# A retention layer and a gated FFN on one core: chunk 4's first and chunk 5's second pair of batches as row tiles, and a new order from chunk 3's end

## The chip, the cores and the metric

The kernel runs on one core of one Trainium2 chip. The metric is the device time of one execution in microseconds (us); the time of a kernel is the median of several runs. Beside the runs there is one profiled execution with a trace of every instruction.

Engines are named as the profile names them: PE is TensorE (matrix products), PEld its loading of the stationary operand, DVE is VectorE, ACT is ScalarE, POOL is GpSimd, SP is SyncE. SP and POOL also issue the transfers.

## The reference

Two stages follow each other. The first is a linear recurrence over 768 positions, for 4 batches and 8 heads of width 64, each head with its own decay:

```
for t in range(S):
    state = gamma * state + k[:, :, t] (outer) v[:, :, t]
    y[:, :, t] = scale * q[:, :, t] @ state
```

The second takes the 3072 rows of 512 values and computes `rms-norm(x) * rms_g`, then `silu(xn @ w_gate) * (xn @ w_val) @ w_out` with an inner width of 1536. Inputs and output are float32; the kernel multiplies in bfloat16.

## The kernel before

The 768 positions are cut into 6 chunks of 128. A chunk c with its 4 batches b is one group of 512 rows: the recurrence is done chunk by chunk, and the FFN of a chunk follows while the recurrence of the next runs in between.

The order of the work is written out by hand. `ORDER` is one long text of words, and the loop at the end calls one small function for each word, in that order; each engine then carries out its own instructions in the order in which they were recorded. A word is a name, then numbers, then `@` with an engine (D, A, P, S for DVE, ACT, POOL, SP) or `/` with the PSUM banks that its products are written to, one digit for each bank. PSUM has eight banks, 0 to 7. A product into a bank waits until the last reader of what stood in that bank is done.

The words that matter here, with c and b as first numbers:

- `Lq`, `Lk`, `Lv` load q, k and v; `Cq` multiplies q by its decay and casts it, `V` does so for v; `tq`, `tk` are transposes on the way of a transfer, issued by SP, that give qT and kT. In chunks 0 and 1 `Tq`, `Tk` transpose on PE and `Eq`, `Ek` copy the result out.
- `A` (L393 to L402) makes the scores of one or two batches, 64 rows of the array high, two heads beside each other in two banks per batch; `M0`, `M1` mask them (L423). `mc` (L276) makes the mask of chunk 1, one half on POOL, one on DVE.
- `Y` (L429 to L443) makes the chunk's output in one bank: 8 products of the masked scores with v, then 4 products of qT with the state `st_b`, 128 rows high.
- `Z` (L405 to L416) makes only the products of qT with the state, for two batches at once, as 16 products 64 rows high that alternate between two banks. Each of the two banks then holds half of the heads of both batches. `Y` with a third number adds the products with v to them (L433). Before, only chunk 4's second pair is done this way.
- `S`, `R`, `N` are the rms norm: squares on ACT, the root on POOL, the scaling on DVE. For a batch that went through `Z`, S and N are two instructions each and R has one more (L452, L464, L476).
- `XE` transposes the normed rows into `xnT`, through SP in the later chunks.
- `K`, `U`, `B` bring the state up to date: products (L525), sum on DVE (L534), cast on POOL (L541).
- `g`, `v` are the FFN's two first products for one of the 12 column blocks (`g.c.n0.n1.b0.b1`, L549), `s` the Silu on ACT (L560), `h` the product with it on DVE (L568, into `hT`).
- `d` is the last product (L575), `e` a part of it for the last batch (L597), `o` the copy out of PSUM (L140), `st` the store (L588).
- `D` (L514) scales k in the first two chunks; `wg`, `wv`, `wo` load the weights through POOL; `H` are products that only keep PE busy at the start.

Rings of buffers in SBUF (the `bufs` in the code) hold an instruction back where its buffer is still in use: 3 for the Silu's result, 4 for `xn`, 6 for `o_sb`.

Of the kernel before, what the change touches and what calls it, by code (L numbers as in the profile page):

```python
# [17 lines left out]
Lk.0.2@S H.4/4 yd causal Lv.0.2@S>causal yt rms.1@S ident Ck.0.2@A Lq.0.0@P H.8/1 Lq.0.1@P Lq.0.2@P Tk.0.2/7 H.3/5  # L18
Lk.0.0@P Tq.0.1/0 vd Tq.0.0/4 Ek.0.2@D Lk.0.1@P Tq.0.2/1 Lk.0.3@P G/7 V.0.2@D Eq.0.1@D Tk.0.0/0 Tk.0.1/6 Eq.0.2@D
Eq.0.0@D iota Lq.0.3@P A.0.2/31 Lv.0.1@P mk0 Lv.0.0@P Lv.0.3@P Ek.0.0@D mk1 GE@A wg.0.2 M1.0.2 wv.0.2 H.2/4 M0.0.2  # L20
Ek.0.1@A A.0.0/5270 D.0.2@P M1.0.1 Tk.0.3/6 Y.0.2/1 Tq.0.3/0 M0.0.1 H.2/4 tab Lk.1.1@P M1.0.0 M0.0.0 S.0.2 Ek.0.3@A
J.0.0/4 J.0.1/7 R.0.2 Y.0.1/2 Eq.0.3@A S.0.1 H.1/6 H.3/0 H.1/5 D.0.0@D Y.0.0/3 N.0.2 J.0.3/5 D.0.1@D wv.2.4 R.0.1
X.0.2/6 N.0.1 S.0.0 wg.2.4 A.0.3/41 R.0.0 X.0.1/0 XE.0.2@A wg.4.6 D.0.3@D M0.0.3 XE.0.1@A g.0.0.2.2.3/2 K.0.2.2/5
K.0.0.2/6 M1.0.3 U.0.2.2@A s.0.0.2.2.3 N.0.0 v.0.0.2.2.3/7 g.0.0.2.1.2/0 h.0.0.2.2.3 Y.0.3/5 Lq.1.0@P wv.4.6 X.0.0/3
U.0.0.2@A S.0.3 wg.6.9 Tk.1.1/4 v.0.0.2.1.2/2 XE.0.0@D s.0.0.2.1.2 h.0.0.2.1.2 g.0.0.2.0.1/6 R.0.3 wv.6.9 Ek.1.1@A
v.0.3.4.0.3/3 v.0.2.3.0.3/4 N.0.3 g.0.3.4.0.3/0 Lk.1.2@P s.0.0.2.0.1 X.0.3/6 v.0.0.2.0.1/5 XE.0.3@A Lk.1.0@P B.0.0
wg.9.12 s.0.3.4.0.3 Lq.1.1@P g.0.5.6.0.3/1 g.0.2.3.0.3/7 h.0.3.4.0.3 s.0.2.3.0.3 Lq.1.2@P h.0.2.3.0.3 g.0.4.5.0.3/0
# [5 lines left out]
g.0.9.10.0.4/4 s.0.9.10.0.4 B.0.2 g.0.10.11.0.4/2 s.0.10.11.0.4 Ek.1.0@D A.1.0/3710 M1.1.1 A.1.2/46 v.0.10.11.0.4/2
v.0.11.12.0.4/0 M0.1.2 M0.1.1 v.0.9.10.0.4/5 M0.1.0 Lv.2.0@S d.0.0.0.4/1 M1.1.0 M1.1.2 h.0.9.10.0.4 Y.1.1/3
d.0.3.0.4/6 Lk.2.3@P h.0.11.12.0.4 Y.1.0/4 S.1.1 Lk.1.3@P R.1.1 h.0.10.11.0.4 S.1.0 N.1.1 d.0.1.0.4/0 R.1.0
d.0.2.0.4/5 N.1.0 X.1.1/3 d.0.2.4.8 d.0.0.4.8 Lv.1.3@P d.0.3.4.8 X.1.0/7 d.0.3.8.12 XE.1.0@A Y.1.2/2 Tq.1.3/7
d.0.0.8.12 S.1.2 d.0.1.4.8 Lq.2.0@S XE.1.1@D o.0.0@A Eq.1.3@D o.0.3@A R.1.2 N.1.2 Tk.1.3/1 d.0.2.8.12 X.1.2/3 Ek.1.3@A
Lk.2.2@P D.1.3@D Lq.2.1@S A.1.3/17 XE.1.2@A M1.1.3 K.1.0/4 K.1.2.2/6 K.1.1/2 B.0.3 M0.1.3 Lq.2.2@S tk.2.2 Lk.2.0@P
g.1.0.1.0.3/3 v.1.2.3.0.3/7 U.1.1@D Y.1.3/1 s.1.0.1.0.3 g.1.1.2.0.3/3 S.1.3 Lk.2.1@P g.1.3.4.0.3/2 o.0.2@A R.1.3
U.1.2.2@D d.0.1.8.12 Cq.2.1@P s.1.3.4.0.3 U.1.0@D g.1.2.3.0.3/2 v.1.0.1.0.3/5 N.1.3 Lq.3.1@S s.1.1.2.0.3 X.1.3/3  # L40
h.1.0.1.0.3 tk.2.0 v.1.3.4.0.3/1 Lk.3.1@P tq.2.1 v.1.1.2.0.3/5 B.1.2 XE.1.3@D h.1.3.4.0.3 s.1.2.3.0.3 h.1.2.3.0.3
h.1.1.2.0.3 g.1.9.10.0.4/4 v.1.9.10.0.4/6 tk.2.3 v.1.0.4.3.4/7 g.1.8.9.0.4/2 Cq.2.0@P Lq.2.3@S o.0.1@D s.1.9.10.0.4
# [30 lines left out]
tk.5.2 Y.4.3.2 Y.4.2.2 S.4.1 h.3.7.8.0.4 v.3.11.12.0.4/7 U.4.0.2@D V.5.1@A tk.5.3 Lv.5.3@S d.3.0.0.10/3 S.4.2 XE.4.0@S
h.3.11.12.0.4 S.4.3 Cq.5.0@P d.3.0.10.12 tq.5.1 R.4.3 N.4.3 o.3.0@A tq.5.0 d.3.2.0.12/1 R.4.1 d.3.1.0.10/2 o.3.2@A
tk.5.1 R.4.2 B.4.0 N.4.1 XE.4.3@S N.4.2 XE.4.2@S V.5.0@D B.4.1 A.5.2/3514 d.3.1.10.12 d.3.3.0.12/6 XE.4.1@S M1.5.2
g.4.8.9.0.4/0 tk.5.0 B.4.3 M1.5.3 M0.5.2 v.4.8.9.0.4/4 o.3.3@D V.5.3@P s.4.8.9.0.4 B.4.2 Y.5.2/5 M0.5.3 o.3.1@A
# [560 lines left out]
```

## Time and profile before

| what | value |
|---|---|
| median of 3 runs | 232.57 us (232.56 to 232.95) |
| profiled execution | 231.72 us |
| its span (first to last instruction) | 230.0 us |
| PE busy | 224.5 us, 98% of the span |
| granted TensorE clock | 1.00 |
| DVE, POOL, ACT busy | 127.3, 105.4, 84.1 us |

In rows of the profile, "L549 PE MATMUL g_ps<-xnT,wg_b 128*128 128x512 x4" is line 549, engine, operation, what is written from what, the size of the stationary tile (rows * columns), the size of the moving operand and how many instructions the row holds. In a stretch in order of time the first two figures are the start and the length in us, and a bracket names the idle time ahead and what ended it. PE's ends are modelled and overlap the next product's start, so a product's slot is read from one start to the next: 0.216 us for 512 columns, 0.056 for 128.

### The profile page before, as it was taken

What the parts mean: (1) busy time and instruction counts of PE and PEld (TensorE: products, weight loads), DVE (VectorE), ACT (ScalarE), POOL (GpSimd) and SP (SyncE); (2) the same over time, 40 slices, a digit from 0 to 9 for tenths busy, and PEclk for the clock granted to TensorE, in tenths of its full rate; (3) what the DMA queues carried; (4) which work ended last, traced back from release to release, by engine and by line L of the source; (5) the groups of instructions that cost most, each with busy time, mean ns of one, the idle gap of its engine ahead of it and who ended that gap; (6) DMA issues with size and microseconds to landing.
All of it is one profiled execution on the core that took longest, in us unless ns stands there. A gap on an engine that the chain in (4) does not pass through costs nothing.

```text
span 230.0 us, 4747 instructions
## 1 busy us (share of the span) xinstructions
PE 224.5 (98%) x1850; PEld 119.0 (52%) x1850; DVE 127.3 (55%) x232; ACT 84.1 (37%) x190; POOL 105.4 (46%) x177
## 2 busy tenths in 40 slices
PE   8889999999999999999999999999999999999994
PEld 3568755556564554444544445544554444444552
DVE  5796497836654876467660538766664325432200
ACT  6776524225423340434410435561354124222021
POOL 8979999327949535636269711338040000000000
PEclk9999999999999999999999999999999999999999
DMA  6999999999999947999899999694117200000142
GB/s 126 175 168 125 189 175 192 200 185 144 125 159 200 180 99 176 212 182 237 181 91 297 148 226 208 138 109 91 49 23 202 98 0 0 0 15 35 45 181 93
DMA packets 105352, 31.51 MB, mean 137 GB/s; under 512 B 94449, under 2 KB 102385, under 8 KB 105330
## 3 DMA queue, kind: packets, MB, share of 16 engines
q1 hardware_dynamic: 65218, 21.51, 45.3%
q0 software_dynamic: 40112, 9.70, 44.9%
q8 instruction: 14, 0.23, 0.4%
q14 instruction: 8, 0.07, 0.1%
HBM read 28.31 MB, written 6.29 MB: 150 GB/s over the span
## 4 chain that ended last, share of the span: by engine, by line
PE 93%; DVE 2%; DMA 2%; POOL 1%; issue 0%; ACT 0%; POOLq 0%; DVEq 0%
PE v_ps L549 27%; PE g_ps L549 27%; PE o_ps L575 26%; PE a_ps L401 2%; PE y_ps L438 2%; DMA qb<-in_q_dram 2%; PE y_ps L442 2%; PE kv_ps L525 1%; PE o_ps L597 1%; PE t_ps L369 1%; PE t_ps L364 1%; DVE am L423 1%; PE xt_ps L492 1%; DVE kd L514 1%; PE g_row_ps L290 0%; DVE xn L479 0%
## 5 line engine op out<-in xcount | busy, mean ns | idle before, releaser
L568 DVE TENSOR_TENSOR hT<-sg,v_ps 128x512 bf16<-128x512 bf16 (+2 forms) x76 | 47.9, 656 | 55.4 <-PE v_ps L549 40.3
L560 ACT ACTIVATE sg<-g_ps 128x512 bf16<-128x512 f32 (+2 forms) x76 | 42.3, 575 | 93.6 <-PE g_ps L549 85.0
L549 PE MATMUL g_ps<-xnT,wg_b 128*128 128x512 bf16 (+2 forms) x344 | 71.2, 344 | 0.0
L549 PE MATMUL v_ps<-xnT,wv_b 128*128 128x512 bf16 (+2 forms) x344 | 71.0, 344 | 0.0
L575 PE MATMUL o_ps<-wo_b,hT 128*128 128x512 bf16 x276 | 63.4, 379 | 0.0
L549 PEld LDWEIGHTS <-wg_b 128*128 128x128 bf16 x344 | 30.7, 98 | 29.6
L549 PEld LDWEIGHTS <-wv_b 128*128 128x128 bf16 x344 | 30.5, 98 | 29.1 <-DVE hT L568 0.2
L575 PEld LDWEIGHTS <-hT 128*128 128x128 bf16 x276 | 26.3, 98 | 29.8
L465 POOL TENSOR_SCALAR ms<-ssq 128x1 f32<-128x1 f32 x24 | 4.5, 188 | 41.2 <-ACT xsq L455 40.3
L423 DVE TENSOR_TENSOR am<-a_ps,causal 128x512 bf16<-128x512 f32 x32 | 20.1, 683 | 3.3 <-PE a_ps L401 3.2
L479 DVE SCALAR_TENSOR_TENSOR xn<-y_ps,rstd,g_bc 128x512 bf16<-128x512 f32 x22 | 16.4, 749 | 9.8 <-POOL rstd L467 8.0
L541 POOL CAST st_b<-st_f 64x256 bf16<-64x256 f32 x40 | 17.7, 443 | 5.4 <-DVE st_f L534 4.1
L455 ACT ACTIVATE xsq<-y_ps 128x512 f32<-128x512 f32 x22 | 13.1, 598 | 15.6 <-PE y_ps L442 14.2
L309 POOL DMA_DIRECT2D kb<-in_k_dram x20 | 18.4, 921 | 0.2 <-issue 0.2
L337 POOL TENSOR_TENSOR qb<-qf,ydec 128x512 bf16<-128x512 f32 x13 | 13.9, 1069 | 7.6 <-DMA qf<-in_q_dram 5.2
L140 ACT COPY o_sb<-o_ps 128x512 f32<-128x512 f32 (+1 forms) x15 | 8.4, 567 | 24.0 <-PE o_ps L575 23.7
L467 POOL TENSOR_TENSOR rstd<-ms,mhalf 128x1 f32<-128x1 f32 x24 | 13.3, 554 | 2.0
L140 DVE COPY o_sb<-o_ps 128x512 f32<-128x512 f32 (+2 forms) x11 | 6.7, 622 | 13.3 <-PE o_ps L575 7.6
L423 DVE TENSOR_TENSOR am<-a_ps,mask 128x512 bf16<-128x512 f32 x16 | 9.9, 683 | 1.7 <-PE a_ps L401 1.6
L356 POOL TENSOR_TENSOR vp<-vf,vdec 128x512 bf16<-128x512 f32 x9 | 9.3, 1045 | 2.4 <-DMA vf<-in_v_dram 2.3
L438 PEld LDWEIGHTS <-am 128*128 128x128 bf16 x176 | 7.7, 98 | 3.5
L234 PE MATMUL hot_ps<-one 128*128 128x512 bf16 x24 | 7.8, 468 | 1.1 <-DVE one L147 1.1
(96 smaller groups left out, 158.5 us busy)
## 6 DMA issues: line engine op xcount, KB each, us to landing
out_dram<-o_sb SPq DMA_DIRECT2D x23, 256.0 KB, 2.4
vf<-in_v_dram SPq DMA_DIRECT2D x17, 256.0 KB, 4.3
qf<-in_q_dram SPq DMA_DIRECT2D x16, 256.0 KB, 5.0
kb<-in_k_dram POOLq DMA_DIRECT2D x23, 128.0 KB, 5.2
wo_b<-in_moe_w_out_dram POOLq DMA_DIRECT2D x3, 512.0 KB, 11.1
qb<-in_q_dram POOLq DMA_DIRECT2D x8, 128.0 KB, 5.7
vp<-in_v_dram POOLq DMA_DIRECT2D x7, 128.0 KB, 5.7
wg_b<-in_moe_w_gate_dram POOLq DMA_DIRECT2D x3, 256.0 KB, 5.7
```

Source lines behind the costliest of these rows:

```text
L140: return (e.copy if e is ACT else e.tensor_copy)(out, in_)
L309: i = done[n, c, b] = e.dma_start(out=x, in_=rows[n][b, c])
L337: e.tensor_tensor(out=u["qb"], in0=u["qf"], in1=ydec[:, c, :, None].to_broadcast([128, H, D]), op=ALU.mult)
L423: return DVE.tensor_tensor(out=u["am"][:, i], in0=u["a"][i], in1=m, op=ALU.mult)
L455: return ACT.activation(xsq, flat(u["y"]), AF.Square, accum_out=u["ssq"])
L467: return POOL.tensor_tensor(out=u["rstd"], in0=ms, in1=mhalf, op=ALU.pow)
L479: return DVE.scalar_tensor_tensor(out=u["xn"], in0=flat(u["y"]), scalar=u["rstd"], in1=g_bc, op0=ALU.mult, op1=ALU.mult)
L541: POOL.tensor_copy(st_b[b][r, :, i * 64:i * 64 + 64], st_f[b // 2][r, b % 2])
L549: r = nc.tensor.matmul(p[:, (n - n0) * m:(n - n0 + 1) * m], W[w][0][:, s, n * 128:(n + 1) * 128], xnT[c][:, s, b0 * C:b1 * C], start=s == ...
L560: return ACT.activation(sg[:, :cols], done["wg", c, n0, b0][:, :cols], AF.Silu)
L568: return DVE.tensor_tensor(out=hT[c][:, n0:n1, b0 * C:b1 * C], in0=sg, in1=p, op=ALU.mult)
L575: nc.tensor.matmul(o_ps[c, b], hT[c][:, n, b * C:(b + 1) * C], wo_b[:, n, :], start=n == 0, stop=n == NFF - 1)
```

## The change

Only `ORDER` changes. It does three things.

First, chunk 4's first pair and chunk 5's second pair of batches get a `Z` word: `Z.4.0/21` stands right behind `A.4.0`, `Z.5.2/60` right ahead of `A.5.2`, and their four `Y` words become `Y.4.0.2`, `Y.4.1.2`, `Y.5.2.2`, `Y.5.3.2`. Chunk 4's second pair keeps its `Z`, chunk 5's first pair stays plain. The norm of these four batches becomes the longer form.

Second, `Lq.5.0`, `Lq.5.1` and `Lv.5.3` stand ahead of `tk.4.3`; some words change engine: `V.4.1` and `V.5.1` from ACT to POOL, `Cq.5.3` from POOL to DVE, and some copies `o` between ACT and DVE.

Third, from `B.3.3` on the words stand in another order, and the banks are dealt anew in all words, from the first line on. Ahead of that place the words and engines are the same as before. One line of the first kind, with only banks changed, and the first lines of the new order:

```
-g.0.7.8.0.4/1 Eq.1.0@D h.0.8.9.0.4 v.0.6.7.0.4/7 h.0.4.6.3.4 wo.8.12 v.0.7.8.0.4/3 s.0.7.8.0.4 h.0.6.7.0.4
+g.0.7.8.0.4/4 Eq.1.0@D h.0.8.9.0.4 v.0.6.7.0.4/6 h.0.4.6.3.4 wo.8.12 v.0.7.8.0.4/0 s.0.7.8.0.4 h.0.6.7.0.4
...
+h.3.4.5.0.4 Lv.4.1@S A.4.0/3604 s.3.10.11.0.4 Z.4.0/21 M1.4.0 M0.4.0 Lq.5.0@S Lq.5.1@S Lv.5.3@S s.3.8.9.0.4 tk.4.3
+v.3.10.11.0.4/5 v.3.8.9.0.4/6 h.3.9.10.0.4 Y.4.0.2 V.5.1@P g.3.7.8.0.4/7 V.4.1@P S.4.0 s.3.7.8.0.4 tk.5.2
```

The words that the prediction speaks of, with the banks of before and of the change: `Y.0.3` 5 and 3, `g.0.3.4` (`g.0.3.4.0.3`) 0 and 3, `Tk.1.2` 2 and 6, `v.0.8.9` 6 and 0, `v.0.6.7` 7 and 6, `v.0.7.8` 3 and 0, `v.0.11.12` 0 and 4, `Y.1.0` 4 and 4, `d.3.0` 3 and 2.

On PE at `v.0.6.7` and `v.0.7.8` in chunk 0 (v_ps_827 and v_ps_834; a bracket names the engines waited for), before:

```order
L549 LDWEIGHTS wg_b_131
L549 MATMUL g_ps_819<-xnT_500,wg_b_131 128x512
L549 LDWEIGHTS wv_b_132
L549 MATMUL v_ps_827<-xnT_500,wv_b_132 128x512
L549 LDWEIGHTS wv_b_132
L549 MATMUL v_ps_827<-xnT_500,wv_b_132 128x512
```

and in the change, where every line number is higher by one:

```order
L550 LDWEIGHTS wg_b_131
L550 MATMUL g_ps_819<-xnT_500,wg_b_131 128x512
L550 LDWEIGHTS wv_b_132
L550 MATMUL v_ps_827<-xnT_500,wv_b_132 128x512 [waits DVE_49]
L550 LDWEIGHTS wv_b_132
L550 MATMUL v_ps_827<-xnT_500,wv_b_132 128x512
```

Nothing has moved there, but the first product of `v.0.6.7` now waits for DVE.

On PE behind chunk 4's first `A` word (a_ps: the scores, kT and qT of batch 1), before:

```order
L401 MATMUL a_ps_2343<-qT_2295,kT_1978 128x128
L401 LDWEIGHTS kT_1978
L401 MATMUL a_ps_2344<-qT_2295,kT_1978 128x128
L549 LDWEIGHTS wv_b_132
L549 MATMUL v_ps_2355<-xnT_2113,wv_b_132 128x512
L549 LDWEIGHTS wv_b_132
```

and in the change:

```order
L402 MATMUL a_ps_2359<-qT_2295,kT_1978 128x128
L402 LDWEIGHTS kT_1978
L402 MATMUL a_ps_2360<-qT_2295,kT_1978 128x128
L415 LDWEIGHTS qT_2272 [waits Activation_49]
L415 MATMUL y_ps_2371<-st_b0_123,qT_2272 128x64 [waits Pool_49]
L415 LDWEIGHTS qT_2272
L415 MATMUL y_ps_2372<-st_b0_123,qT_2272 128x64 [waits Pool_49]
```

The 16 products of `Z.4.0`, of which the first two are shown, have come between the scores and the FFN's `v.3.10.11`.

On DVE between the state's sums of chunk 4 (st_f) and the first copies of chunk 3's output, before:

```order
L534 TENSOR_TENSOR st_f1_122<-st_f1_122,kv_ps_2495 128x512
L568 TENSOR_TENSOR hT_2227<-sg_2514,v_ps_2559 128x512
L534 TENSOR_TENSOR st_f0_121<-st_f0_121,kv_ps_2521 128x512
L568 TENSOR_TENSOR hT_2227<-sg_2519,v_ps_2586 128x512
L476 SCALAR_TENSOR_TENSOR xn_2639<-y_ps_2539,rstd_2637,g_bc_116 128x4x64
L476 SCALAR_TENSOR_TENSOR xn_2639<-y_ps_2540,rstd_2637,g_bc_116 128x4x64
```

and in the change:

```order
L535 TENSOR_TENSOR st_f0_121<-st_f0_121,kv_ps_2528 128x512
L535 TENSOR_TENSOR st_f1_122<-st_f1_122,kv_ps_2509 128x512
L477 SCALAR_TENSOR_TENSOR xn_2611<-y_ps_2371,rstd_2554,g_bc_116 128x4x64
L477 SCALAR_TENSOR_TENSOR xn_2611<-y_ps_2372,rstd_2554,g_bc_116 128x4x64
L569 TENSOR_TENSOR hT_2227<-sg_2434,v_ps_2614 128x512
L477 SCALAR_TENSOR_TENSOR xn_2631<-y_ps_2556,rstd_2609,g_bc_116 128x4x64
```

`N.4.1` (xn_2611, out of the two banks of `Z.4.0`) now stands ahead of the FFN's `h.3.7.8` and of `N.4.3`; before, `N.4.3` (xn_2639) came first, behind both `h` words.

More of the change, by code (lines that the diff above doesn't have):

```diff
@@ L17 @@
 ORDER = """
[L18 to L27, printed above, removed]
@@ L33 @@
[L33 to L42, printed above, removed]
@@ L73 @@
[L73 to L76, printed above, removed]
-A.5.0/2067 Y.5.3/3 S.5.3 h.4.8.9.0.4 g.4.0.1.0.4/4 M0.5.1 M1.5.1 v.4.7.8.0.4/1 M1.5.0 M0.5.0 g.4.7.8.0.4/7 S.5.2
@@ L88 @@
-v.5.4.5.0.4/5 g.5.4.5.0.4/7 h.5.2.3.0.4 s.5.5.6.0.4 v.5.5.6.0.4/2 d.4.1.0.10/0 d.4.1.10.12 h.5.8.9.0.4 s.5.4.5.0.4
-g.5.10.11.0.4/6 d.4.0.0.10/7 s.5.10.11.0.4 h.5.4.5.0.4 g.5.1.2.0.4/5 v.5.1.2.0.4/3 h.5.5.6.0.4 o.4.1@D s.5.1.2.0.4
-h.5.1.2.0.4 v.5.10.11.0.4/4 d.4.0.10.12 st.4.1@S d.5.0.0.10/6 d.4.2.0.12/1 h.5.10.11.0.4 o.4.0@A o.4.2@D e.5.3.2/5
-o.5.3.2@D d.5.0.10.12 d.4.3.0.12/2 st.4.0@S d.5.1.0.10/0 o.4.3@A st.4.3@S o.5.0@D st.5.0@S d.5.1.10.12 e.5.3.1/6
-o.5.1@A st.4.2@S o.5.3.1@D d.5.2.0.12/0 st.5.3.2@S st.5.1@S st.5.3.1@S e.5.3.0/1 o.5.2@A st.5.2@S o.5.3.0@A st.5.3.0@S
+Lk.0.2@S H.4/0 yd causal Lv.0.2@S>causal yt rms.1@S ident Ck.0.2@A Lq.0.0@P H.8/1 Lq.0.1@P Lq.0.2@P Tk.0.2/0 H.3/1
@@ new lines @@
+s.1.8.9.0.4 h.1.0.4.3.4 g.1.5.6.0.4/7 Lv.2.1@S B.1.1 h.1.8.9.0.4 v.1.5.6.0.4/5 s.1.5.6.0.4 g.1.4.5.0.4/7
+g.1.10.11.0.4/0 Cq.3.1@D Lv.2.2@S v.1.11.12.0.4/1 Cq.2.3@P h.1.5.6.0.4 s.1.11.12.0.4 B.1.3 h.1.11.12.0.4
+v.1.10.11.0.4/5 s.1.10.11.0.4 s.1.4.5.0.4 h.1.10.11.0.4 v.1.4.5.0.4/7 Cq.3.0@P h.1.4.5.0.4 g.1.7.8.0.4/1 Lk.3.0@P
+A.2.0/5024 tq.2.3 tq.2.2 M0.2.0 v.1.7.8.0.4/7 Lv.2.3@S tq.3.1 Lk.3.2@P M0.2.1 s.1.7.8.0.4 M1.2.1 g.1.6.7.0.4/5
+h.1.7.8.0.4 M1.2.0 V.2.1@P v.1.6.7.0.4/2 Y.2.1/7 s.1.6.7.0.4 S.2.1 K.2.1/0 tk.3.1 K.2.0/5 V.2.2@P h.1.6.7.0.4
@@ L93 @@
+h.5.1.2.0.4 d.4.0.10.12 g.5.2.3.0.4/5 v.5.5.6.0.4/1 s.5.5.6.0.4 s.5.10.11.0.4 d.4.3.0.12/3 s.5.8.9.0.4 h.5.5.6.0.4
+h.5.8.9.0.4 s.5.2.3.0.4 o.4.0@D v.5.10.11.0.4/7 d.4.1.0.10/5 h.5.2.3.0.4 d.5.0.0.10/0 h.5.10.11.0.4 e.5.3.1/7
+d.5.0.10.12 st.4.0@S d.5.1.0.10/2 o.4.3@A o.5.0@A d.4.1.10.12 d.5.1.10.12 st.5.0@S e.5.3.2/0 o.5.1@A o.4.1@D o.5.3.2@A
+d.4.2.0.12/5 st.4.3@S st.5.1@S o.4.2@D o.5.3.1@D st.5.3.2@S st.4.1@S d.5.2.0.12/0 e.5.3.0/7 o.5.2@A st.5.3.1@S
+o.5.3.0@A st.4.2@S st.5.2@S st.5.3.0@S
 """
```

106 lines of the change are left out of this document (62 added, 44 removed).

## The prediction

> **What bounds the kernel now.** I read the page first, then the waits of PE, then stretches of time, then single stretches in order of time.
>
> ```profile
> span 230.0 us, 4747 instructions
> PE 224.5 (98%) x1850; PEld 119.0 (52%) x1850; DVE 127.3 (55%) x232; ACT 84.1 (37%) x190; POOL 105.4 (46%) x177
> PE 93%; DVE 2%; DMA 2%; POOL 1%; issue 0%; ACT 0%; POOLq 0%; DVEq 0%
> ```
>
> PE is busy for 98% of the span and holds 93% of the chain that ended last; no other engine is above 55%. The next rows are PE's waits, all of them.
>
> ```profile
> PE hot_ps L234 <- DVE one L147: 1.1, 1, 1.1
> PE t_ps L364 <- DMA qb<-in_q_dram: 0.6, 1, 0.6
> PE xt_ps L492 <- DVE xn L479: 0.4, 1, 0.4
> PE t_ps L364 <- DVE am L423: 0.2, 1, 0.2
> ```
>
> All four lie before 17 us. The table of stretches shows the group where the order is made anew:
>
> ```profile
> 137.00:170.00 33.00, 33.00 (x322) 17.42 (x321) 22.82 (x37) 14.55 (x46) 11.71 (x26) 1.00 0.60 110
> ```
>
> Its first figures are the length and PE's busy time: 33.00 of 33.00, at a granted clock of 1.00. So from 17 us to the last product the kernel's time is PE's products laid end to end. A change can win only by taking product time away, and every wait that it adds on PE is paid in full, for nothing later is idle and could take it up.
>
> **The row tiles.** Plain and row-tiled products stand side by side before:
>
> ```profile
> 145.04 0.41 PE L438 MATMUL y_ps<-vp,am 128*128 128x64 bf16 x8
> 145.50 1.03 PE L549 MATMUL g_ps<-xnT,wg_b 128*128 128x512 bf16 x4
> 148.38 0.41 PE L414 MATMUL y_ps<-st_b,qT 64*128 64x64 bf16 x16
> 148.72 1.04 PE L549 MATMUL v_ps<-xnT,wv_b 128*128 128x512 bf16 x4
> 149.60 0.63 PE L433 MATMUL y_ps<-vp,am 128*128 128x64 bf16 x16
> 150.06 1.03 PE L549 MATMUL v_ps<-xnT,wv_b 128*128 128x512 bf16 x4
> 158.36 0.62 PE L401 MATMUL a_ps<-qT,kT 64*128 64x128 bf16 x16
> 158.91 3.19 PE L575 MATMUL o_ps<-wo_b,hT 128*128 128x512 bf16 x14
> ```
>
> I count from start to start, since the ends are modelled. A plain Y word takes 145.50 - 145.04 = 0.46 us, a pair 0.92. The Z word of chunk 4's second pair took 148.72 - 148.38 = 0.34, and the two Y words behind it 150.06 - 149.60 = 0.46. An A word of 16 products, also 64 rows high, takes 0.55 before PE is back on full height; about 0.11 of that, as of the 0.34, I put down to the way back. Two new pairs get Z words, and both stand directly against an A word (Z.4.0 behind A.4.0, Z.5.2 ahead of A.5.2), so they share its way in and out and cost 0.34 - 0.11 = 0.23. A pair then takes 0.23 + 0.46 = 0.69 where it took 0.92: **-0.46** for two. If the sharing fails a pair saves 0.12, together 0.24; more than 0.46 nothing in the rows gives. The Trainium skill, "TensorE: Matmul & The Clock Gate", section "Wait — 56ns, not 53.3ns?", says that products never start less than about 25 ns apart however small they are. By it 16 products take 0.40 us, a pair saves 0.06 and the forecast rises by 0.34; the row of 16 in 0.34, way back included, speaks against the rule for row tiles that run side by side.
>
> **The banks.** Up to chunk 3 the words keep their order, but nearly every PSUM bank is dealt anew, from the first line on. A product into a bank waits until the bank's last reader is done. So I laid the new bank numbers over the old times: for each product, when did the bank's new last tenant get its last reader? Where that is later than the product's start, PE will wait. Most places have tenths to spare. The first real one is g.0.3.4 in bank 3, behind Y.0.3, whose last reader is N.0.3:
>
> ```profile
> 21.06 0.56 POOL L467 TENSOR_TENSOR rstd<-ms,mhalf 128x1 f32<-128x1 f32 x1
> 21.66 0.75 DVE L479 SCALAR_TENSOR_TENSOR xn<-y_ps,rstd,g_bc 128x512 bf16<-128x512 f32 x1 [0.73 <-POOL rstd L467]
> 21.91 0.81 PE L549 MATMUL g_ps<-xnT,wg_b 128*128 128x384 bf16 x4
> ```
>
> N.0.3 waits for the rstd that GpSimd makes between weight loads, whatever PE does, and ends at 21.66 + 0.75 = 22.41. The g products start at 21.91: **+0.50**. Two smaller waits of the same kind at 19 us are swallowed by this one, since it ends at a fixed time. Queued behind it on PE is all the rest.
>
> The second place is where Vector falls behind:
>
> ```profile
> 29.42 2.34 DVE L276 TENSOR_TENSOR mask<-causal,vdec 128x512 f32<-128x512 bf16 x1
> 30.14 1.06 POOL L514 TENSOR_TENSOR kd<-kb,vdec 128x512 bf16<-128x512 bf16 x1
> 31.13 1.84 POOL L309 DMA_DIRECT2D vp<-in_v_dram  x2
> 31.77 1.44 DVE L514 TENSOR_TENSOR kd<-kb,vdec 128x512 bf16<-128x512 bf16 x1
> 33.07 1.89 PE L549 MATMUL v_ps<-xnT,wv_b 128*128 128x512 bf16 x8
> 33.13 0.41 DVE L140 COPY kT<-t_ps 128x512 bf16<-128x512 bf16 x1
> 34.06 0.67 DVE L568 TENSOR_TENSOR hT<-sg,v_ps 128x512 bf16<-128x512 bf16 x1
> 34.80 1.03 PE L549 MATMUL g_ps<-xnT,wg_b 128*128 128x512 bf16 x4
> ```
>
> The row of eight v products is v.0.6.7 (33.07) and v.0.7.8 (four products later, 33.07 + 4 x 0.216 = 33.94). In the new dealing v.0.6.7 takes bank 6 behind Tk.1.2, whose reader is the kT copy (ends 33.54), and v.0.7.8 takes bank 0 behind v.0.8.9, whose reader is the hT product (ends 34.06 + 0.67 = 34.73). Moved on by 0.50 the first stands at 33.57 and is free to go; the second stands at 34.44 and waits 34.73 - 34.44 = **+0.29**, provided that Vector's stretch keeps its times. I take that it does: the mask product takes 2.34 us, its twin on GpSimd (next fence) 1.04, and it ends 0.56 behind GpSimd's kd, so it looks held by GpSimd, whose own queue does not move with PE.
>
> ```profile
> 28.32 1.04 POOL L276 TENSOR_TENSOR mask<-causal,vdec 128x512 f32<-128x512 bf16 x1
> 35.72 0.38 PE L369 MATMUL t_ps<-ident,kb 128*128 128x128 bf16 x4
> 35.94 0.76 PE L369 MATMUL t_ps<-ident,qb 128*128 128x128 bf16 x8
> 36.53 1.24 PE L549 MATMUL g_ps<-xnT,wg_b 128*128 128x512 bf16 x5
> 42.69 1.87 DVE L568 TENSOR_TENSOR hT<-sg,v_ps 128x512 bf16<-128x512 bf16 x3
> 43.92 0.40 PE L438 MATMUL y_ps<-vp,am 128*128 128x64 bf16 x8
> ```
>
> Something is given back: before, the transposes at 35.72 start 0.05 late (34.80 + 4 x 0.216 = 35.66), and the twelve of them take 36.53 - 35.72 = 0.81 where 12 x 0.056 = 0.67 are needed. Their new banks are free earlier: **-0.20**. At 43.92 Y.1.0 takes bank 4 behind v.0.11.12, whose reader is the second of three hT products from 42.69 (42.69 + 0.60 + 0.68 = 43.97): **+0.05**. From there to 137 us the new dealing has about ten places with less than 0.1 us to spare, each good for a few hundredths; together between 0 and 0.5, and I take **+0.25**.
>
> **The new order from chunk 3's end.** Adding the slots word by word, PE's work from there is the same but for the row tiles, with as many changes of tile height. I looked at what each product needs. One place falls short: d.3.0 in bank 2, which held the pair of Z.4.0 and is free only when both of its batches are through S, R and N.
>
> ```profile
> 147.75 0.70 PE L525 MATMUL kv_ps<-vp,kb 128*64 128x64 bf16 x32
> 151.63 0.40 ACT L452 ACTIVATE xsq<-y_ps 128x256 f32<-128x256 f32 x1
> 153.70 0.88 DVE L476 SCALAR_TENSOR_TENSOR xn<-y_ps,rstd,g_bc 128x256 bf16<-128x256 f32 x2 [1.81 <-POOL rstd L467]
> 161.94 1.03 PE L549 MATMUL g_ps<-xnT,wg_b 128*128 128x512 bf16 x4
> 163.01 0.60 ACT L560 ACTIVATE sg<-g_ps 128x512 bf16<-128x512 f32 x1 [6.12 <-PE g_ps L549]
> ```
>
> From S to the end of N a row-tiled batch took 153.70 + 0.88 - 151.63 = 2.95 us. S.4.1 stands behind the Silu of g.3.11.12, which starts 163.01 - 161.94 - 0.86 = 0.21 behind its products and takes 0.60. So bank 2 is free 0.21 + 0.60 + 2.95 = 3.76 us after g.3.11.12. PE reaches d.3.0 after one Y (0.23), the K products and their way in (0.63 + 0.09), Z (0.34), two Y (0.46) and two v words (1.73): 3.48. **+0.3**; nothing if ACT overlaps the Silu's end, and 0.9 if one more Vector product comes between. The V products that go from ACT to GpSimd (two) and the Cq from GpSimd to Vector have no product waiting for them within 2 us. The loads pulled up land earlier; what SP has to issue ahead of chunk 5's transposes is the third rival. The end, an e word, ACT copy and store, is the same.
>
> **Sum.** -0.46 + 0.50 + 0.29 - 0.20 + 0.05 + 0.25 + 0.30 = +0.73. The profiled execution took 231.72, of which 230.0 is the span; 1.72 around it stays. That makes 232.45 for such an execution, and as the median of the runs shown is 232.57, 0.85 above it, the forecast is 232.57 + 0.73 = **233.3 us**.
>
> **Rivals.** First: Vector's stretch is not held by GpSimd but moves with PE. Then the kT copy ends at 33.54 + 0.50 = 34.04 against v.0.6.7 at 33.57 (0.47), and the hT product at 35.23 against v.0.7.8 at 34.91 (0.32): 0.79 in place of 0.29, **233.8**. For it: Vector's work there starts from a Silu that PE feeds. Against it: the length of 2.34. The Trainium skill, "SBUF — State Buffer", section "Who interferes with whom", says that of a Vector product with two SBUF inputs and a GpSimd instruction that reads SBUF, whoever issues first holds the shared port for all of it. The mask product is on record first, 29.42 against 30.14, which would favour this rival; its 2.34 against kd's 1.06 does not.
>
> Second, the side that is not slower: the 0.50 moves Vector's mask and kd products off GpSimd's, and they take 1.04 and 0.68 (as hT) in place of 2.34 and 1.44. It decides once the stretch ends 0.29 earlier. Then the wait at 34 goes, and with Vector 2 us ahead the 0.30 of small releases up to 137: 233.3 - 0.59 = **232.7**. For it: such products do vary this much; against: both lie in the densest part of GpSimd's queue.
>
> Third, the transposes of chunk 5 come late.
>
> ```profile
> 159.17 1.22 SPq L385 DMA_TRANSPOSE kT<-kb  x1
> DMA to landing us min/median/max: 2.4/4.0/7.6
> ```
>
> The new order puts four of them behind XE.4.2. The last xn of chunk 4 is there about 15.5 us after A.4.0 by the chain above; its own transpose and three more at 1.22 put the last issue at 20.4 and its landing, by the median of 4.0 (those that write qT), at 24.4. A.5.0's turn is at 25. A landing at 5 to 7.6 costs 0.4 to 3.0: around **234.6**.
>
> **How the numbers follow.** Forecast 0.45, first rival 0.28, second 0.15, third 0.12. The range has to reach from the second rival with bank 2 free in time (232.4) over the first with bank 2 at 0.9 (234.4) to the middle of the third: 232.4 to 234.6. A measurement of this kernel tells about 0.2%, 0.47 us, from no change: slower means above 233.04. That is three quarters of the forecast's cases, nearly all of the first and third rival's, and few of the second's: slower 0.76, same 0.19, faster 0.05 (every wait at nothing leaves -0.46).
>
> **What would show it.** In the new profile PE should wait for Vector near 22 us (0.5) and near 34.5 (0.3, or 0.8 by the first rival, or nothing by the second), run 0.6 late at 40 us, and have a 0.3 us gap before d.3.0. The 32 new row-tiled products should stand beside A words at 0.23 a pair. If PE shows no wait at 22 us, the reading of the banks is wrong, and with it the sign.

## The result, and the profile after

The changed kernel takes 233.09 us (median of 22 runs, 232.37 to 234.94), the kernel before 232.19 in as many runs beside it (231.47 to 232.95). The ratio (over the runs, not just of the two medians) is 1.0048, with a 95% interval of 1.0030 to 1.0066: slower by half a per cent, 0.90 us. The forecast was 233.3, in a range of 232.4 to 234.6. What the medians don't show is that the runs have drawn apart: the middle half of them lies between 231.9 and 232.5 before, and between 232.5 and 234.2 after.

The profiled execution took 232.38, one of the quick ones. Its page opens with these lines, then come the shares of the chain that ended last:

```profile
span 230.7 us, 4747 instructions
PE 223.4 (97%) x1839; PEld 119.0 (52%) x1866; DVE 127.0 (55%) x237; ACT 80.5 (35%) x182; POOL 107.2 (46%) x182
PE 89%; POOL 4%; issue 2%; SPq 1%; DVE 1%; DMA 1%; ACT 1%; POOLq 0%
```

The span is 0.7 longer. A few records of PE are missing (1839 products in place of 1866), so its busy time can't be compared; starts can. SP's queue and ACT have come into the chain. All of PE's waits (us in all, times, the longest):

```profile
PE hot_ps L235 <- DVE one L148: 1.1, 1, 1.1
PE a_ps L402 <- ACT o_sb L141: 0.8, 1, 0.8
PE xt_ps L493 <- DVE xn L480: 0.5, 1, 0.5
PE g_ps L550 <- issue: 0.2, 1, 0.2
PE o_ps L576 <- issue: 0.2, 1, 0.2
```

The first and the third (0.4 there) were there before. The second is new, and no term of the forecast: a scores product waits 0.8 for a copy of FFN output. (The two of 0.2 are gaps of one missing product.) In order of time, on PE:

```profile
161.32 2.75 PE L576 MATMUL o_ps<-wo_b,hT 128*128 128x512 bf16 x12
163.91 0.63 PE L434 MATMUL y_ps<-vp,am 128*128 128x64 bf16 x16
165.37 0.62 PE L402 MATMUL a_ps<-qT,kT 64*128 64x128 bf16 x16 [0.83 <-ACT o_sb L141]
```

`A.5.0/2537` takes bank 2, where `d.3.0` stood; the copy that empties it is `o.3.0`, on ACT:

```profile
161.52 0.60 ACT L561 ACTIVATE sg<-g_ps 128x512 bf16<-128x512 f32 x1 [5.05 <-PE g_ps L550]
164.73 0.59 ACT L141 COPY o_sb<-o_ps 128x512 f32<-128x512 f32 x1 [2.61 <-DMA out_dram<-o_sb]
```

The copy waited 2.61 for a store to land, since all six `o_sb` buffers were taken. The stores and transposes on SP's own queue, first of the changed kernel:

```profile
147.03 0.58 SPq L589 DMA_DIRECT2D out_dram<-o_sb  x1
147.71 8.54 SPq L499 DMA_TRANSPOSE xnT<-xn  x4
156.34 1.21 SPq L386 DMA_TRANSPOSE kT<-kb  x1
157.65 2.53 SPq L386 DMA_TRANSPOSE qT<-qb  x2
160.28 2.02 SPq L386 DMA_TRANSPOSE kT<-kb  x1
162.40 1.00 SPq L589 DMA_DIRECT2D out_dram<-o_sb  x2
```

then of the kernel before:

```profile
134.20 0.53 SPq L588 DMA_DIRECT2D out_dram<-o_sb  x1
...
136.69 0.57 SPq L588 DMA_DIRECT2D out_dram<-o_sb  x1
```

The row at 162.40 holds `st.2.3` and `st.2.1`. Before, `st.2.3` was the row at 134.20. In the new order it stands behind the four `XE.4` and four transposes of chunk 5, 28 us later, and lands 2.3 us after its issue, at 164.73, where the copy starts. The row of the four `XE.4` takes 8.54, where four issues of 1.2 would take 4.9: SP also stands there until chunk 4's normed rows are ready, and the store stands behind that as well. So the chain is: transposes on SP, store, buffer, copy, bank 2, scores.

### The profile page after: what moved, and what is told of

It reads as the page before. It is cut to its first block, busy times and chain, and to the rows that moved or that the text cites. A ratio compares the mean times of both kernels' runs of the same rounds, so it can differ in the third digit from the quotient of the medians.

```text
span 230.7 us, 4747 instructions
## 1 busy us (share of the span) xinstructions
PE 223.4 (97%) x1839; PEld 119.0 (52%) x1866; DVE 127.0 (55%) x237; ACT 80.5 (35%) x182; POOL 107.2 (46%) x182
## 4 chain that ended last, share of the span: by engine, by line
PE 89%; POOL 4%; issue 2%; SPq 1%; DVE 1%; DMA 1%; ACT 1%; POOLq 0%
PE g_ps L550 26%; PE v_ps L550 26%; PE o_ps L576 21%; PE hot_ps L235 4%; PE a_ps L402 3%; PE y_ps L439 2%; SPq L386 1%; PE y_ps L443 1%; POOL st_b L542 1%; PE o_ps L598 1%; PE kv_ps L526 1%; PE t_ps L370 1%; DMA out_dram<-o_sb 1%; PE t_ps L365 1%; POOL qb L338 1%
## 5 line engine op out<-in xcount | busy, mean ns | idle before, releaser
L550 PE MATMUL g_ps<-xnT,wg_b 128*128 128x512 bf16 (+2 forms) x336 | 70.1, 343 | 0.5 <-issue 0.2
L550 PE MATMUL v_ps<-xnT,wv_b 128*128 128x512 bf16 (+2 forms) x334 | 69.8, 343 | 0.4
L576 PE MATMUL o_ps<-wo_b,hT 128*128 128x512 bf16 x267 | 62.4, 379 | 0.5 <-issue 0.2
L480 DVE SCALAR_TENSOR_TENSOR xn<-y_ps,rstd,g_bc 128x512 bf16<-128x512 f32 x18 | 13.5, 748 | 8.5 <-POOL rstd L468 6.7
L141 ACT COPY o_sb<-o_ps 128x512 f32<-128x512 f32 (+2 forms) x15 | 8.1, 548 | 25.7 <-PE o_ps L576 22.7
L456 ACT ACTIVATE xsq<-y_ps 128x512 f32<-128x512 f32 x18 | 10.7, 596 | 14.8 <-PE y_ps L443 13.6
L338 POOL TENSOR_TENSOR qb<-qf,ydec 128x512 bf16<-128x512 f32 x12 | 12.9, 1071 | 5.3 <-DMA qf<-in_q_dram 2.6
L357 POOL TENSOR_TENSOR vp<-vf,vdec 128x512 bf16<-128x512 f32 x11 | 11.4, 1046 | 7.6 <-DMA vf<-in_v_dram 7.4
L141 DVE COPY o_sb<-o_ps 128x512 f32<-128x512 f32 (+1 forms) x11 | 7.0, 655 | 14.2 <-PE o_ps L576 14.2
L402 PE MATMUL a_ps<-qT,kT 64*128 64x128 bf16 x192 | 7.6, 217 | 0.8 <-ACT o_sb L141 0.8
```

The costliest lines, as they stand in the source:

```text
L141: return (e.copy if e is ACT else e.tensor_copy)(out, in_)
L338: e.tensor_tensor(out=u["qb"], in0=u["qf"], in1=ydec[:, c, :, None].to_broadcast([128, H, D]), op=ALU.mult)
L402: nc.tensor.matmul(u["a"][i][:, hp, :], u["kT"][r, hp, :], u["qT"][r, hp, :], start=True, stop=True)
L480: return DVE.scalar_tensor_tensor(out=u["xn"], in0=flat(u["y"]), scalar=u["rstd"], in1=g_bc, op0=ALU.mult, op1=ALU.mult)
L550: r = nc.tensor.matmul(p[:, (n - n0) * m:(n - n0 + 1) * m], W[w][0][:, s, n * 128:(n + 1) * 128], xnT[c][:, s, b0 * C:b1 * C], start=s == ...
L576: nc.tensor.matmul(o_ps[c, b], hT[c][:, n, b * C:(b + 1) * C], wo_b[:, n, :], start=n == 0, stop=n == NFF - 1)
```

## The experiments

The **store theory** says that this chain makes the loss and the spread. The **transpose rival** is the prediction's third: A.5.0 waits for chunk 5's q and k. Each kernel is compared with the kernel before on the same chip. Three chips were used, and a difference between two experiments below is that of their medians as they stand:

| kernel | median us (lowest to highest, runs) | before | ratio, 95% interval |
|---|---|---|---|
| e1 store ahead | 231.82 (231.57 to 232.94, 13) | 232.16 | 0.9977, 0.9959 to 0.9995 |
| e2 seven buffers | 231.80 (231.60 to 232.46, 12) | 232.16 | 0.9984, 0.9970 to 0.9999 |
| e3 new front banks alone | 232.26 (231.78 to 233.19, 12) | 232.16 | 1.0008, 0.9990 to 1.0025 |
| e9 one bank | 232.10 (231.82 to 233.43, 12) | 232.16 | 0.9997, 0.9979 to 1.0015 |
| e4 e1 without row tiles | 232.46 (231.88 to 233.48, 11) | 232.07 | 1.0019, 1.0005 to 1.0033 |
| e5 e1 with old front banks | 231.60 (231.09 to 232.42, 12) | 232.07 | 0.9987, 0.9974 to 1.0001 |
| e7 e1 with late loads | 232.07 (231.46 to 232.78, 12) | 232.07 | 0.9994, 0.9971 to 1.0016 |
| e8 e1, row tiles apart, first form | 236.35 (234.88 to 237.98, 6) | 232.07 | 1.0187, 1.0153 to 1.0220 |
| e10 e1, row tiles apart | 232.33 (231.82 to 234.50, 12) | 232.16 | 1.0010, 0.9986 to 1.0033 |
| e11 one store ahead of it | 233.14 (232.55 to 234.03, 12) | 232.16 | 1.0036, 1.0018 to 1.0055 |
| e12 three stores ahead of it | 232.95 (232.04 to 233.87, 12) | 232.16 | 1.0033, 1.0013 to 1.0052 |
| e13 e5 with seven buffers | 231.67 (231.48 to 232.18, 11) | 232.16 | 0.9979, 0.9964 to 0.9995 |

### e1 and e2: the store ahead, or a seventh buffer

e1 moves one word, e2 changes one number:

```
 S.4.3 B.4.2 R.4.3 N.4.1 v.3.7.8.0.4/6 st.1.2@S
+st.2.3@S
...
 Y.5.2.2 s.4.8.9.0.4 tq.5.1 tk.5.1
-st.2.3@S
```

```
-            done["o", c, b] = ring([128, DM], F32, "o_sb", 6)
+            done["o", c, b] = ring([128, DM], F32, "o_sb", 7)
```

> The changed kernel, with one word moved: the store of chunk 2's fourth batch is issued right behind that of chunk 1's third, ahead of chunk 4's transposes of xn and chunk 5's of q and k, instead of behind them. Store theory: in the changed kernel's trace A.5.0 stands 0.9 us, because its bank is emptied by a ScalarE copy that waited 2.61 us for an o_sb buffer, which this store gives free only when it has landed. Then the wait before A.5.0 goes, the median falls by 0.9 from 233.1 to about 232.2, and the runs lie within 1.5 us as those of the kernel before do, not within 2.6. Transpose rival (the third one of the prediction): A.5.0 waits for chunk 5's q and k, which are transposed late; then nothing changes, or 0.5 more is lost, as the store now stands ahead of them: 233.1 to 233.6.

> The changed kernel with a ring of seven o_sb buffers instead of six; its order is not touched. Store theory: the copy o.3.0 gets the seventh buffer and no longer waits for the store of chunk 2's fourth batch; the wait before A.5.0 goes though the store is as late as before, and the median falls to about 232.2. A theory that the store itself, as traffic or as an issue ahead of something, is what costs: no gain here, 233.1. Transpose rival: 233.1 as well, and then e1 shows none either.

Both come to 231.8, 1.3 under the changed kernel, and the middle half of their runs lies within 0.3 and 0.5 us. In e1 SP issues the store together with `st.1.2`,

```profile
148.47 1.06 SPq L589 DMA_DIRECT2D out_dram<-o_sb  x2
```

and the scores follow the Y products without a gap:

```profile
165.34 0.63 PE L434 MATMUL y_ps<-vp,am 128*128 128x64 bf16 x16
165.91 0.62 PE L402 MATMUL a_ps<-qT,kT 64*128 64x128 bf16 x16
```

In e2 the store is as late as ever; here is its row on SP's queue, and the copy on ACT:

```profile
162.45 1.00 SPq L589 DMA_DIRECT2D out_dram<-o_sb  x2
```

```profile
162.30 0.58 ACT L141 COPY o_sb<-o_ps 128x512 f32<-128x512 f32 x1
```

The copy now starts 0.15 ahead of the store that it had waited for. Two ways that share nothing but the buffer take the loss away, and the transposes stand where they stood: the store theory holds and the transpose rival falls. The gain of 1.3 is larger than the wait of 0.83 in the trace, which is of a quick execution, and with the wait the spread is gone as well. That the slower executions waited longer fits this, but no trace of a slow one of the changed kernel was taken.

### e11 and e12: the store later

```
-st.2.3@S
+st.2.1@S st.2.3@S
...
-st.2.1@S
```

for e11; in e12 `st.2.1`, `st.2.0` and `st.2.2` come ahead of it.

> The changed kernel with chunk 2's second batch's store issued ahead of the fourth's instead of behind it: the store that the copy o.3.0 waits for is 0.58 us later (one issue of 0.5 to 0.6 on SP). Store theory: the wait before A.5.0 grows from 0.9 to 1.5 in a trace and the median by 0.58, 233.1 to 233.7. If not this store but chunk 5's transposes held A.5.0: 233.1, as they are not moved.

> The same with three stores of chunk 2 ahead of it: 3 x 0.58 = 1.74 later. Store theory: a wait of 2.7 before A.5.0, and a median of 234.8. Some runs of the changed kernel had a mean granted clock of 0.992 and of e8 0.991 to 0.993: if a longer wait lets the clock fall behind it, half the clock over some 3.5 us costs another 1.7, and the median goes to 236 or 237 with a mean clock near 0.992.

Both expectations miss: 233.1 and 233.0, as the changed kernel. e11's copy on ACT and its stores on SP's queue:

```profile
166.32 0.58 ACT L141 COPY o_sb<-o_ps 128x512 f32<-128x512 f32 x1 [2.94 <-DMA out_dram<-o_sb]
```

```profile
164.04 1.05 SPq L589 DMA_DIRECT2D out_dram<-o_sb  x2
```

and e12's:

```profile
164.74 0.58 ACT L141 COPY o_sb<-o_ps 128x512 f32<-128x512 f32 x1 [2.10 <-DMA out_dram<-o_sb]
```

```profile
162.04 2.33 SPq L589 DMA_DIRECT2D out_dram<-o_sb  x4
```

The copy starts 166.32 - 164.04 = 2.28 and 164.74 - 162.04 = 2.70 behind the first store of the group, whichever it is. `st.2.3`, the second and the fourth there, can't have landed by then: the fourth was issued some 164.74 - 163.9 = 0.8 before. So the ring doesn't hand out one fixed buffer; the copy gets that of the store which comes first in the order. My edit exchanged stores behind the last transpose, and the first store kept its place. By these rows it counts when the first store of that group is issued, and no run here moves that one later. Three stores issued earlier cost nothing that the medians tell. Nor did the clock fall, as e12's expectation allowed: none of the 24 runs of e11 and e12 has a mean granted clock below 0.998.

### e3, e9 and e5: the banks of the front

e3 puts the new banks up to `g.3.10.11` into the kernel before, and e5 the old ones into e1; in both the banks behind are only renamed. e9 is the prediction's first term alone: in the kernel before, banks 0 and 5 are exchanged from `g.0.3.4` on.

```
-X.0.0/3
+X.0.0/5
...
-g.0.3.4.0.3/0
+g.0.3.4.0.3/3
```

is e3 at two of its words, and

```
-g.0.3.4.0.3/0
+g.0.3.4.0.3/5
```

the first word that e9 touches.

> The kernel before with only the bank numbers of the changed kernel up to chunk 3's last g words; from there its own order, its banks renamed so that they fit. By the prediction's own terms: 0.50 + 0.29 - 0.20 + 0.05 + 0.25 = +0.89, 233.1. By the changed kernel's trace: PE 0.35 late at 22 us, nothing at 34, 0.13 late at 36.5 and 0.23 at 44, which stays: 232.45, +0.25. If dealing the banks anew costs nothing in the median: 232.2.

> The kernel before with banks 0 and 5 exchanged from g.0.3.4 on: the one new wait is g.0.3.4 behind Y.0.3, whose reader N.0.3 ended at 22.41 us where the g products started at 21.91. Every wait on PE is paid in full: a wait of 0.50 at 22 us and 0.45 to 0.50 at the end, 232.65. Later stalls take it up (before, the transposes near 36 us stood 0.2 for their banks, and these do not move): 0.50 at 22 us, 0.25 or less from 37 us on, 232.4.

> The kernel of e1 with the banks of the kernel before up to chunk 3's last g words, the later banks renamed so that they fit: row tiles, new order and early store, without the new front. By the changed kernel's trace the front's banks cost 0.23, so 231.6; by the medians of e3 (0.1 above the kernel before) 231.7; by the prediction's terms for the front (0.89) 230.9.

The new front costs 0.1 by e3 against the kernel before (its interval reaches from -0.2 to +0.6 us), and 0.2 by e1 against e5 (231.82 - 231.60): of the prediction's 0.89 for it little is in the medians. e9's wait is there, 0.4 in its list of PE's waits, but the median does not move:

```profile
PE g_ps L550 <- DVE xn L480: 0.4, 1, 0.4
PE t_ps L365 <- DVE am L424: 0.2, 1, 0.2
```

The traces of all kernels tell why. Each execution enters the front at another time (ten of the fourteen lists of PE's waits have one for q there), so I set starts against that of `A.0.2`, PE's first scores (the row of 8 a_ps products near 10 us):

| | A.0.2 | g.0.3.4 | A.1.0 | K.3.2 | from A.0.2 to K.3.2 |
|---|---|---|---|---|---|
| before | 9.89 | 21.91 | 38.36 | 117.54 | 107.65 |
| old banks: e5, e13 | 9.92, 10.58 | 22.24, 22.60 | 38.72, 39.27 | 117.90, 118.45 | 107.98, 107.87 |
| e9 | 9.68 | 22.25 | 38.48 | 117.67 | 107.99 |
| new banks: after, e3 | 9.97, 10.09 | 22.26, 22.37 | 38.48, 38.60 | 117.81, 117.93 | 107.84, 107.84 |
| e2, e4, e7 | 9.94, 10.40, 10.19 | 22.23, 22.70, 22.48 | 38.77, 39.24, 39.02 | 118.10, 118.58, 118.35 | 108.16, 108.18, 108.16 |
| e8, e10, e12 | 10.11, 10.03, 10.20 | 22.40, 22.32, 22.50 | 38.94, 38.83, 39.00 | 118.28, 118.17, 118.34 | 108.17, 108.14, 108.14 |
| e1, e11 | 10.44, 10.41 | 22.73, 22.70 | 39.92, 39.74 | 119.25, 119.08 | 108.81, 108.67 |

The trace of before, from which I worked, happens to have the shortest front; with the same banks e5 and e13 take 0.2 to 0.3 more. e9 enters `g.0.3.4` 0.55 later than before (12.57 after A.0.2, against 12.02), but then reaches `A.1.0` in 16.23, where the three traces with the old banks take 16.45 to 16.67. So `A.1.0` comes 28.80 after A.0.2, with the old banks 28.47, 28.69 and 28.80: the wait is paid at 22 us and at least in part given back by 38. And the new front has three cases, which part between `g.0.3.4` and `A.1.0`: 16.22 and 16.23 in two (after, e3); 16.50 to 16.54 in six; 17.04 and 17.19 in two. In time they are the second rival, the forecast and the first rival. The changed kernel's own trace, of the first case, on DVE:

```profile
29.75 1.81 DVE L277 TENSOR_TENSOR mask<-causal,vdec 128x512 f32<-128x512 bf16 x1
31.88 0.69 DVE L515 TENSOR_TENSOR kd<-kb,vdec 128x512 bf16<-128x512 bf16 x1 [0.32 <-DMA kb<-in_k_dram]
```

e2's, of the second, on DVE and on PE:

```profile
31.47 1.50 DVE L515 TENSOR_TENSOR kd<-kb,vdec 128x512 bf16<-128x512 bf16 x1
```

```profile
34.55 1.02 PE L550 MATMUL v_ps<-xnT,wv_b 128*128 128x512 bf16 x4 [0.15 <-DVE hT L569]
```

and e1's, of the third:

```profile
32.68 1.45 DVE L515 TENSOR_TENSOR kd<-kb,vdec 128x512 bf16<-128x512 bf16 x1 [0.64 <-DMA kb<-in_k_dram]
```

```profile
34.51 1.02 PE L550 MATMUL v_ps<-xnT,wv_b 128*128 128x512 bf16 x4 [0.47 <-DVE kT L141]
35.70 1.02 PE L550 MATMUL v_ps<-xnT,wv_b 128*128 128x512 bf16 x4 [0.17 <-DVE hT L569]
```

What parts them is when Vector's kd product ends: 22.5 to 22.6 us after A.0.2 in the first case, 23.0 in the second, 23.5 and 23.7 in the third. That hangs on when chunk 1's k lands (kd waits 0.64 for it in e1, 0.76 in e11) and on how long Vector's mask and kd products take: 1.8 and 0.7 in the first case, 1.8 and 1.3 to 1.5 or 2.6 and 0.7 in the second.

### e4, e8 and e10: the row tiles

e4 takes the two new row tiles out of e1, e10 moves them one word away from their A words:

```
-Z.4.0/21
...
-Y.4.0.2
+Y.4.0/2
...
-Y.4.1.2
+Y.4.1/1
...
-Z.5.2/60
...
-Y.5.2.2
+Y.5.2/6
...
-Y.5.3.2
+Y.5.3/0
```

```
 A.4.0/3604 s.3.10.11.0.4
-Z.4.0/21
...
 v.3.10.11.0.4/5
+Z.4.0/21
...
-d.3.0.10.12 B.4.3 Z.5.2/60 A.5.2/3714
+B.4.3 Z.5.2/60 d.3.0.10.12 A.5.2/3714
```

> The kernel of e1 (changed kernel, store ahead) with the two new row tiles undone: chunk 4's first and chunk 5's second pair take plain Y words again, each in a bank of its own; the rest of the order stays. By the prediction's count two pairs cost 0.46 us more: from e1's 231.8 to 232.3. If the sharing of the way in and out with the A words were worth nothing, 0.24 more: 232.05. In the trace the only new waits on PE would be ones of the plain pairs.

> The kernel of e1 with both new row tiles one word away from their A word: Z.4.0 behind the next v word, Z.5.2 ahead of the last d word before A.5.2, so that each changes the tile height by itself. By the prediction's count the sharing is worth 0.11 a pair: 0.22 more, 232.05. By the traces' rows a change to 64 rows costs 0.10 and the one back 0.11, both of which A pays anyway: 0.41 more, 232.2.

> As e8, but the cast B.4.3 stays ahead of Z.5.2, so that every product reads what it should: the kernel of e1 with Z.4.0 one word behind A.4.0, and Z.5.2 one word ahead of A.5.2. By the prediction's count the sharing is worth 0.11 a pair: e1's 231.8 + 0.22 = 232.05. By the rows of e8 around Z.4.0 (0.095 more on the way to 64 rows, 0.108 on the way back): 231.8 + 0.41 = 232.2, which is nearly what taking the row tiles out costs.

Without them 0.64 is lost by the medians, with them apart 0.51; the terms of 0.46 and 0.41 lie within what these medians tell apart, so the rows decide. The changed kernel's rows on PE around `Z.4.0`, then e10's:

```profile
139.70 0.62 PE L402 MATMUL a_ps<-qT,kT 64*128 64x128 bf16 x16
140.16 0.40 PE L415 MATMUL y_ps<-st_b,qT 64*128 64x64 bf16 x16
140.49 1.90 PE L550 MATMUL v_ps<-xnT,wv_b 128*128 128x512 bf16 x7
```

```profile
140.05 0.62 PE L402 MATMUL a_ps<-qT,kT 64*128 64x128 bf16 x16
140.60 1.04 PE L550 MATMUL v_ps<-xnT,wv_b 128*128 128x512 bf16 x4
141.57 0.41 PE L415 MATMUL y_ps<-st_b,qT 64*128 64x64 bf16 x16
141.91 1.04 PE L550 MATMUL v_ps<-xnT,wv_b 128*128 128x512 bf16 x4
```

Beside A, from A to full height takes 140.49 - 139.70 = 0.79, against 0.55 for A alone (140.60 - 140.05): the row tile costs 0.24. Apart it costs 141.91 - 141.57 = 0.34, and 141.57 - 140.60 - 4 x 0.216 = 0.11 on the way in: 0.45. So standing beside A is worth 0.21 a pair (the new row at chunk 5, `Z.5.2` ahead of `A.5.2`, shows the same 0.24: 159.04 - 158.80), and a row tile by itself, 0.45 + 0.46 for its two Y words, saves nothing against the 0.92 of plain ones.

In e8 I had put `Z.5.2` ahead of `B.4.3` too: it reads the state as it was before that update. Its time says nothing on row tiles, but shows the third rival at work. GpSimd and PE:

```profile
159.51 0.86 POOL L542 CAST st_b<-st_f 64x256 bf16<-64x256 f32 x2 [4.82 <-PE y_ps L415]
160.45 1.04 POOL L338 TENSOR_TENSOR qb<-qf,ydec 128x512 bf16<-128x512 f32 x1
```

```profile
165.36 0.40 PE L402 MATMUL a_ps<-qT,kT 64*128 64x128 bf16 x8
168.09 0.40 PE L402 MATMUL a_ps<-qT,kT 64*128 64x128 bf16 x8 [2.34 <-DMA kT<-kb]
```

`B.4.3` had to wait 4.82 until Z had read; the cast of q behind it on GpSimd came at 160.45 (156.44 in e1, whose execution was 1 us later by K.3.2), the transposes with it, and A.5.0 stood 2.34 for kT.

### e7 and e13: the loads, and a combination

e7 puts the three loads of e1 back, `Lq.5.1` behind `d.2.0`, `Lq.5.0` behind `A.4.2`, `Lv.5.3` behind `tq.5.3`. e13 is e5 with seven buffers.

> The kernel of e1 with the three loads that the change pulled up (q of chunk 5's first and second batch, v of its fourth) put back where the kernel before had them in the order of work: behind the first words of chunk 2's last d, behind A.4.2 and behind the transpose tq.5.3. If the loads only land earlier than anyone needs them, 231.8 as e1, within 0.2. If the earlier loads keep the later casts and transposes in time, a wait comes before A.5.0 and 0.3 or more is lost.

> The kernel of e5 (old front banks, row tiles, new order, early store) with seven o_sb buffers, so that no copy waits for a store at all. If the early store already took away every such wait: 231.6, as e5, and below the kernel before (232.1) by 0.2%. If late stores still cost in some runs: 231.3 and a narrower spread.

e7's 232.07 is 0.25 above e1, and no wait stands ahead of A.5.0 in its trace; the intervals overlap, so no effect of the loads is shown. e13, at 231.67, is as e5. The medians of e13 and e5 lie some 0.5 under the kernel before. The interval of e13 (0.9964 to 0.9995) keeps clear of 1, that of e5 (0.9974 to 1.0001) just reaches it: the change without its late store and with the old front banks is faster than the changed kernel, and by e13 a little faster than the kernel before.

## Why the prediction was right, and where it was wrong

The time and the sign were right, and nearly by accident: against the medians the front was taken 0.7 too dear, 0.3 was added for a wait at d.3.0 that did not come, and a late store that costs 1.3 was not seen. The absolute time had luck too: it stood on a median of three runs, 232.57, where 22 runs gave 232.19.

- **The row tiles, -0.46: right.** 0.24 in place of 0.23 beside A. The share of it that comes from standing beside A was mis-sized: 0.21, not 0.11. The Trainium skill, "TensorE: Matmul & The Clock Gate", section "Wait — 56ns, not 53.3ns?", has products start at least about 25 ns apart; the trace disagrees for these products of two row tiles, 16 of them in 0.24 us, 15 ns each.
- **g.0.3.4, +0.50: the mechanism was right, the size 0.27.** From A.0.2 to g.0.3.4 the changed kernel takes 12.29 where the kernel before took 12.02 (e13, with the old banks, 12.02 too; e5 12.32, where PE's weights landed late). The prediction's sign, a wait for Vector near 22 us, is not in the changed kernel's list, and by the prediction's own rule the reading of the banks would be wrong. e9 shows that it was right, with a wait of 0.39 at that product. In the changed kernel PE is already 0.16 late from the small waits at 19 us (20.85 - 9.97 against 20.61 - 9.89), and at g.0.3.4 only 0.11 is left to wait, (22.26 - 20.85) - (21.91 - 20.61). The products just ahead of it, in the kernel before:

```profile
20.61 1.46 PE L549 MATMUL v_ps<-xnT,wv_b 128*128 128x384 bf16 x8
```

and in the changed kernel, with it:

```profile
20.85 1.46 PE L550 MATMUL v_ps<-xnT,wv_b 128*128 128x384 bf16 x8
22.26 0.81 PE L550 MATMUL g_ps<-xnT,wg_b 128*128 128x384 bf16 x4
```

  N.0.3 did not end at a fixed time: Tq.0.3 no longer waits in its new bank (the wait of 0.2 for `am` is gone from the list), so a Y product (13.62, before 13.82), ACT's squares and GpSimd's queue behind them (14.83, before 15.04) ran 0.2 earlier, and so N.0.3:

```profile
21.45 0.75 DVE L480 SCALAR_TENSOR_TENSOR xn<-y_ps,rstd,g_bc 128x512 bf16<-128x512 f32 x1 [0.36 <-POOL rstd L468]
```

  I had costed the new waits of the dealing and passed over an old one that it ended, some 9 us ahead.
- **Every wait that the change adds is paid in full: not borne out in the front.** Of e9's 0.39 at 22 us between nothing and 0.33 is left at A.1.0, by which trace of the old banks it is set against, and its median does not move.
- **Vector's stretch, +0.29 and -0.20: right in six of ten traces** (16.50 to 16.54 against 16.45). Two have the first rival's time and two the second's, the changed kernel's own trace among them, but not for the rivals' reasons: in the first rival's traces Vector waits for k and not for PE, and in the second's the mask product still takes 1.81 and only kd is short. The Trainium skill, "SBUF — State Buffer", section "Who interferes with whom", says that a Vector product with two SBUF inputs contends with a GpSimd instruction that reads SBUF, that issue order decides who blocks, and, of Vector's two-port modes, that whoever issues first has the shared ports for its whole instruction. The rows bear out that the two contend, and not that the first one wins: the mask product on Vector came first, at 29.75, and took 1.81, while GpSimd's kd behind it kept its length. In e13, the one trace of fourteen in which GpSimd's kd starts only when the mask has ended (30.83, behind 30.10 + 0.69), the mask takes 0.69. The changed kernel's row on GpSimd:

```profile
29.94 1.06 POOL L515 TENSOR_TENSOR kd<-kb,vdec 128x512 bf16<-128x512 bf16 x1
```

- **Y.1.0 and the small places, +0.05 and +0.25: 0.15 together** (A.1.0 to K.3.2 takes 79.33 to 79.34 in all ten traces with the new banks, 79.18 to 79.19 in the four others).
- **d.3.0, +0.30: nothing.** The changed kernel's N.4.1 on DVE, and PE's row:

```profile
150.18 0.88 DVE L477 SCALAR_TENSOR_TENSOR xn<-y_ps,rstd,g_bc 128x256 bf16<-128x256 f32 x2 [0.28 <-POOL rstd L468]
```

```profile
150.93 7.93 PE L576 MATMUL o_ps<-wo_b,hT 128*128 128x512 bf16 x36
```

  The two N products read one bank each, the first of them bank 2, which is free after half of this row, near 150.18 + 0.44 = 150.62, and d.3.0 goes at 150.93. I had waited for both.
- **The step that failed:** "The loads pulled up land earlier; what SP has to issue ahead of chunk 5's transposes is the third rival." I followed SP's queue up to the transposes and not past them. Behind them stood `st.2.3`, 28 us later than before, and on its buffer hang the copy `o.3.0`, bank 2 and A.5.0. The third rival had the place and the queue right, but not the victim: the transposes had time in hand (e8 held them back by some 5 us for a wait of 2.3). Nothing in the working asked when each `o_sb` buffer is free.
- **The sum of the profiled executions:** +0.27 at K.3.2, -0.46, and 0.89 ahead of A.5.0 (165.37 - 163.91 = 1.46 from the Y products on, against 165.91 - 165.34 = 0.57 in e1) make +0.70; the spans differ by 0.7. The +0.27 at K.3.2 belongs to a front of the first case; of the nine other traces with the new banks one took the same and eight took 0.3 to 1.0 more.

What stays open: why the wait at A.5.0 changes between executions (0.83, 1.16 and 0.31 in the three traces with the store behind the transposes), and so why the runs spread to 234.94. The wait alone does not make the difference between two executions: e11's trace is 1.6 longer than the changed kernel's, of which 0.33 is the wait, 0.83 the front and 0.44 a later start of it. By the middle half of the runs the spread is 1.7 in the changed kernel, 1.0 and 1.1 in e11 and e12, and 0.3 to 0.7 in the other experiments, e8 apart, and in the kernel before; so the wide spread comes with the copy that waits for the late store, and e1 and e2 take it away. What moves the store, and how front and store act together, is not shown.

## What to carry to other kernels

When an order of work is made anew, follow each queue past the transfers that somebody visibly waits for: a store has a reader too, the next user of its buffer, and with a short ring a store issued late is a wait on the engine that empties PSUM, then on the bank, then on TensorE. A bank dealt otherwise takes waits away as well as adding them, and in a front that is paced by loads both are partly swallowed. One order of work gave fronts 0.3 us apart with the old banks and 1.0 apart with the new, so price such a front from several executions. A row tile paid here only beside other work of its height.
